# Fused attention and gated convolution on one core: first batch loaded in six-token rows, 120-query tiles, 48-row last tiles, and another written-out order

## The chip, the cores and the metric

The kernel runs on one core of a Trainium2 chip. The metric is device time in microseconds (us), lower is better. Three timed runs of the kernel before gave 172.52, 176.39 and 176.44, median 176.39. One further execution was profiled.

A core has TensorE (PE; its weight loads stand in the profile as PEld), VectorE (DVE), ScalarE (ACT), GpSimd (POOL), which here mostly issues DMAs that convert fp32 to f16 on the way, and SyncE (SP), which only issues DMAs. Each works through its own list in order; semaphores join them.

## The reference

```python
def _attn_ref(q, k, v, n_global, n_local):          # 4 x 8 heads x 768 x 64; 8 global keys, window 96
    scores = scale * np.matmul(q, k.transpose(0, 1, 3, 2))
    rel = pos[:, None] - pos[None, :]
    is_global = pos[None, :] < int(n_global)
    is_local = (rel >= 0) & (rel < int(n_local))
    dist = np.where(is_global & ~is_local, float(n_local), np.abs(rel).astype(np.float32))
    scores = np.where(is_global | is_local, scores - slopes[:, None, None] * dist, -1e9)
    a = np.exp(scores - np.max(scores, axis=-1, keepdims=True))
    return np.matmul(a / (np.sum(a, axis=-1, keepdims=True) + 1e-09), v)

def _moe_ref(x, w_proj, filter_fft, w_out):         # x: 4 x 768 x 512, the heads side by side
    x1, x2, x3 = np.split(x @ w_proj, 3, axis=-1)
    X2 = np.fft.rfft(x2, n=S, axis=1)
    Hf = np.fft.rfft(filter_fft, n=S, axis=0)[None]
    return (x1 * np.fft.irfft(X2 * Hf, n=S, axis=1) * x3) @ w_out
```

Attention keeps a key if it is among the first 8 or at most 95 positions back, with a slope per head times the distance. Its output is projected to x1, x2 and x3; x2 is convolved along the sequence with a filter, multiplied by the other two, and projected again.

## The kernel before

**Tiles of attention.** Keys are cut into seven tiles (`K0`). A tile has 128 partitions: the 8 global keys and 120 keys of its own (`KL`). Tile 6 begins at token 648, so that it is full; only its last 48 keys are new. Scores are computed transposed, keys on partitions and queries along the row. Key tile m meets the queries from 120m on, 216 of them (`EW`: 168 and 48 for the last two). `QT` holds the queries of a batch as one row of 768 per head pair, `KT` the keys by tile and head pair. `scores` (L671) makes two matmuls per tile and head pair, one per head, each on 64 rows of the array (L693). The tiles come in three groups c (`GRP`: tiles 0-1, 2-3, 4-6), so a batch has 12 score operations (4 head pairs by 3 groups), each followed by one exponential on ACT over 864 elements (L707). `values` (L727) multiplies by V with a column of ones, DVE takes reciprocals and scales (`xn`, L766), `transpose_x` (L776) turns the result into `xT`.

**The bias.** In batch 0 it is added by matmuls ahead of the scores (L684): `slope` (diagonals with the heads' slopes) times `near` (distances, spread from `dg`, which POOL makes with iota and affine_select in `distances`, L475). In batches 1 to 3 DVE multiplies the exponentials by `mask` (L724), eight tables of 648 that ACT makes once (L543).

**How q and k come in.** For batch 0, SP loads q as fp32, six tiles of 128 queries into `ot`; PE transposes them as fp32 (`turned32`, L633). POOL loads k and V by `load_run`, one DMA per tile of 960 pieces of 256 bytes (120 keys by 8 heads). For batches 1 and 2, POOL loads q, k and V (`load_rows`, `load_q`, L322), and PE transposes tiles one or two at a time (`turned`, L645). For batch 3 (`CROSS`), SP transposes from buffer to buffer by DMA: three for k, by group, and six for q (`crossed`, L620). All batches share `qn`, `kn`, `QT` and `KT`, so a load waits until the batch before has been transposed.

**The convolution.** `gate` (L846) makes x1 and x3 (two times four matmuls of 384 columns, L856), an eviction of each on ACT or DVE, and their product on DVE. `butterfly` (L794) combines thirds of `xT`; projections (L925), forward transforms (L613), products on DVE, inverse transforms (L950, L953) and the output projection (L977) follow. `ot` is the eviction of the output and SP stores it (L985), one DMA of 128 x 512 fp32 per tile.

**Setup.** DVE builds `rows` (integers 0 to 127 and multiples) by doubling; PE makes angles from them and ACT sines (`tables`). Slopes are 16 ACT operations on 64 x 64 diagonals (L528). DVE fills ones and zeros.

**The order.** `ORDER` is a list written out by hand. Each word is the number of an operation in the order in which `graph` makes them, the engine that runs it (P, A, V, G for POOL, S for SP) and the PSUM banks that it takes; `i13b1` are 13 filler matmuls on `idle` into bank 1. Eight banks exist; an operation that takes a bank waits for all that read the bank's last contents. Each engine works through its own words in this order.

Of the kernel before, what the change touches and what calls it, by code (L numbers as in the profile page):

```python
# [39 lines left out]
0V 42V 3V 7V 27S 59S 28S 60S 61S 26S 69S 4G 54A 48A 45A 56A 50A 5V 1V 6V 29G 30G 66G 33G 65G 77G i6b1 17P0 18A  # L40
58A 47A 46A 43A 19V 11V 12P1 13A 49A 44A 57A 2A 14V 8V 15V 16A 55A 53A 20V 34V 39A 21A 51A 52A 22A 36A 37A 10V
40V 35G 70G 71G 72G 32G 68G 67G 73G i15b3 120P2 121V 9V 41V 93P3 94A 97P1 98V 82V 38V 258G 31G 74G 75G 267G
266G 226P0 95P4 96A 99A 230A 100P5 i1b6 122P2 123A 87A i1b1 126P3 127V 231V 269G i2b1 124P4 125V 101V 62V 64V
229V 268G 257G 255G 256G 259G 79G 76G 78G 80G 81G 262G i2b1 128P67 129A 134P23 135A 91P1 92V 24V 63V 132P45
133A 130P67 131A 102P23 103A 168P1 169V 227V 106P45 107A 170P6 171V 232V 166P7 167A 172P1 173V 228V 25V 261S
260S 263S 264S 275G 274G 273G 272G 265G 104P23 105A 108P45 109A 176P67 177A 178P01 179A 86A 136P23 137V 138V
141P45 142V 143V 174P67 175A 83A 115P23 116V 117V 110P01 111V 112V 180P45 181A 139P6 140A 89A 88A 144P7 145V
182P23 183V 184V 118P0 119A 85A 113P1 114V 187P45 188V 189V 383P7 185P6 186A 84A 384A 385P2 386V 213V 152P3
190P4 191V 212V 219V 215V 220V 357P6 147P2 149A 358A 154A 355P5 356V 198P4 200A 90A 359P2 360V 222V 214V 488G
271G 270G 496G 487G 489S 484G 495G 485G 193P7 195A 162P3 164A 396P01 397A 398V 216V 221V 364P45 361P67 362A  # L50
365A 208P2 210A 151P3 153V 366V 223V 23V 224V 225V 217V 146P0 148A 161P1 163A 165V 150V 218V 157P4 159A 370P67
393P23 394A 395V 367P01 368A 371A 192P5 194V 369V 372V 196V 156P4 158A 160V 155V 363V 233V 234V 235V 236V 237V
238V 239V 297P2 295P3 296A 387P01 388A 298A 390P67 280P4 281A 293P3 294A 391A 207P0 299P1 308P2 309A 300A
306P3 307A 301P5 203P4 205A 302A 284P2 285A 431P1 429P3 430A 432A 202P4 204V 209V 433P5 434A 490S 504G 486G
277G 503G 501G 276G 278G 506G 502G 494G 498G 378P67 379V 380V 392V 389V 252P23 253A 254A 240P4 241V 244P1 245A
246P5 247A 248P67 250A 249A 242P0 243A 373P23 374V 375V 206V 211V 719G 282P1 435P45 436A 283A 399P67 400V 401V
251V 441P23 442A 197P0 199A 404P45 405V 310V 406V 722G 491G 493S 720S 492S 381P1 382V 376P6 377A 288P7 289A
402P2 403V 443V 286P0 287A 583P3 407P4 408A 585P5 586V 437V 290V 584V 291V 303V 438P67 439A 440V 304V 292V
444P01 587P2 588A 445A 446V 311V 715G 717S 716G 409P4 419P5 410P6 412A 421A 420P7 595P23 596A 422A 598P01 599A
425P6 424P5 426A 427A 411A 447P23 448V 305V 449V 611P7 612A 723G 497G 279G 452P01 453V 454V 728G 505G 714G  # L60
500G 659P6 660A 324P5 314P4 315A 320P7 321V 428V 600V 312P2 316P3 317A 325A 313A 450P6 661P4 662A 318P0 455P3
456V 423V 201V 451V 478V 477V 413V 597V 479V 326P5 327A 319A 322P7 415P1 417A 323A 589P23 592P45 593A 811S
414P6 416A 468P0 470A 590A 458P1 460A 613P7 614V 418V 480V 328V 329V 481V 482V 594V 330V 483V 331V 591V 332V
457P6 459A 657P0 658A 729G 507G 734G 713G 712G 499G 730G 726G 727G 725G 732G 731G 724G 735G 733G 473P2 475A
618P45 619A 620V 333V 335V 621P67 615P01 616A 622A 463P3 472P2 474A 462P4 464A 465A 512P5 513A 521P6 522A
669P01 670A 624P23 625A 626V 525P7 526A 523P6 524A 672P45 663P01 664A 508P2 509A 673A 601P67 602V 334V 603V
623V 336V 665V 617V 671V 510P3 511A 467P0 536P1 537A 666P45 667A 668V 838S 718S 814S 813S 812S 837S 882S 721S
839S 883S 340P2 341A 469A 514P1 516P3 517A 515A 632P67 604P2 534P0 535A 538V 633V 674V 527P4 528A 605A 343P3
344A 606P01 607V 634V 608V 518V 352P5 353A 354S 529P4 530A 675P23 676V 519V 471V 635P5 636A 677A 627P67 609P4
610V 680P01 681V 628V 629V 532V 682V 531V 539V 520V 533V 346P5 337P4 338A 347A 339S 345S 342S 348S 349P6 630P7  # L70
631A 821P23 824P01 825A 350A 822A 351S 678P4 679V 826V 683P5 638P7 640A 684A 705V 653P0 548P6 546P1 547A 549A
550P2 544P3 554P7 555A 551A 545A 552P4 553V 706V 708V 707V 466V 461V 709V 476V 542P1 543A 655A 686P5 688A
691P4 693A 643P2 645A 540P3 541A 556V 843P67 840P01 841A 849P45 850A 647P2 649V 637P3 639A 844A 652P0 654V
823V 557V 558V 710V 559V 842V 560V 641V 711V 701P1 703A 893P45 846P23 847A 894A 815P67 736P0 737A 816A 817V
648P1 650A 749P2 890P45 891A 750A 696P3 698A 762P0 763A 832P67 833V 563V 651V 834V 561V 848V 892V 564V 753P1
754A 642P4 644A 751P5 752A 887P23 888A 884P01 818P67 819A 820V 845V 851V 895V 656V 740P4 741A 764P5 738P2 739A
885A 765A 766V 695P3 697A 700P4 742P2 743A 827P67 828V 829V 889V 886V 562V 757P0 758A 580P5 581A 702A 744P1
685P0 687A 755P5 756A 830P4 831A 745A 857P23 858V 859A 896P67 897V 898V 901P45 902V 903A 746V 747V 760V 689V
568P0 565P1 852P67 853V 854V 759V 748V 767V 571P2 572A 577P3 578A 860P4 690P5 861V 761V 835P2 836A 566A 855P3
856A 904P6 905A 899P7 900V 927V 926V 646V 929V 928V 930V 931V 704V 932V 574P2 575A 576S 567S 573S 582S 768P1  # L80
782P4 770P6 771A 569A 570S 579S 774P3 780P2 778P7 779A 783A 769A 868P6 776P0 777A 775A 772P7 773A 781A 784V
785V 786V 699V 787V 788V 791V 862P4 950P1 951A 933P7 934A 692A 694V 789V 792V 937P0 948P1 949A 938A 946P5
935P7 936A 947A 954P1 955A 867P0 952P3 959P5 961P7 962A 869A 953A 960A 872P1 874V 957V 956V 958V 963V 964V
941P2 942A 864A 870A 917P7 939P0 940A 943V 944V 945V 802P1 803A 805P5 878P6 863P4 865A 877P0 980P1 981V 866V
790V 971P4 972A 919A 879A 880A 808P3 984P4 978P2 982P7 983A 979A 967P1 968V 985V 986V 965P0 966A 969P6 970A
973V 881V 974V 975V 987V 976V 988V 977V 1004V 989V 799P7 793P4 794A 800A 801S 795S 804S 873P6 875A 809A 876V
871V 916P2 918A 796P1 797A 991V 990V 992V 993V 994V 920V 1006V 798S 810S 921P4 912P0 914A 911P3 913A 806A 923A
807S 922P2 906P1 908A 924A 925V 915V 907P3 909A 910V 1007V 1005V 1001P0 1002A 1003S 995P1 996A 997S 998P2 999A
1000S 1008P0 1009V 1010S 1014P1 1015V 1016S 1011P3 1012A 1013S
# [108 lines left out]
class Fused:  # L198
# [11 lines left out]
    CROSS = (3,)  # L210
    LATER = ()
# [8 lines left out]
    def __init__(self, ctx, tc, q, k, v, n_global, n_local, w_proj, filt, w_out, out):  # L220
# [10 lines left out]
        self.K0 = [KL * t for t in range(6)] + [S - KL]  # L231
# [6 lines left out]
    def buffers(self):  # L238
# [5 lines left out]
        self.qn = t("qn", [P, 6, H, D])  # L244
        self.kn = t("kn", [P, 7, H, D])
        self.vn = [t(f"vn{i}", [P, 7, H, self.VD]) for i in range(2)]
        self.QT = t("QT", [P, 4, S])
# [4 lines left out]
        self.xn = [t(f"xn{i}", [P, 2, 7, 2, D]) for i in range(2)]  # L252
# [12 lines left out]
        self.h1 = t("h1", [P, 6, DM])  # L265
        self.h2 = t("h2", [P, 6, DM])
# [24 lines left out]
        self.wide_dg = self.mix.bitcast(BF16).rearrange("p a b c -> p (a b c)")[:, 0:648]  # L291
        self.cst = t("cst", [1, 4])
        self.one = t("one", [1, P])
# [31 lines left out]
    def load_rows(self, what, dst, src, b, t):  # L325

        lo, hi = self.K0[t], self.K0[t] + KL
        self.load("G", dst[P - (hi - lo):P, t, :, 0:self.D],
                  src[b, :, lo:hi, :].rearrange("h p d -> p h d"), [what + (t,)], (8 * (hi - lo), 256),
                  f"load{what}{t}")  # L330

    def load_run(self, what, dst, src, t, n):

        rows = src[0, :, self.K0[t]:self.K0[t] + KL * n, :].rearrange("h (t p) d -> p t h d", t=n)
        self.load("G", dst[NG:P, t:t + n, :, 0:self.D], rows, [what + (i,) for i in range(t, t + n)],
                  (8 * KL * n, 256), f"load{what}{t}")

    def load_q(self, b, t):
        src = self.q[b, :, P * t:P * t + P, :].rearrange("h p d -> p h d")
        if b == 0:  # L340
            st = self.ot[t].rearrange("p (h d) -> p h d", h=self.H)
            self.load("S", st, src, [("ot", t)], (1024, 256), f"q{t}")
            if self.Q32:
                return
            self.g.op("AV", {"A": act(512), "V": 0.7}, lambda e: self.copy(
# [26 lines left out]
    def setup(self):  # L372
# [6 lines left out]
        def rows(_):  # L379
            row = self.row  # L380
            v.memset(row[:, 4, 0:1], 0.0)
            for n in (1, 2, 4, 8, 16, 32, 64):
                v.tensor_scalar(row[:, 4, n:2 * n], row[:, 4, 0:n], float(n), None, op0=Alu.add)
# [857 lines left out]
```

## Time and profile before

| | |
|---|---|
| timed runs | 172.52, 176.39, 176.44 us (median 176.39) |
| the profiled execution | 173.44 us, span 171.7 us |
| busy: PE, DVE, ACT, POOL | 162.3, 156.7, 151.1, 77.4 us |
| granted TensorE clock, mean | 0.998 |
| first exponential of batch 0 | starts at 17.50 us |
| first gate matmul | starts at 31.2 us |
| last load issued by POOL | ends at 91.6 us |
| last eviction of the output | 167.88 to 168.48 us |

The span runs from the first to the last instruction of the program; the time has a little around it. Times in lines are microseconds from the start of the span. A group's line ends with its count, the busy time in us, the mean of one in ns, and the engine's idle time ahead of them with what ended it. An engine's instructions overlap, so their durations add up to more than the time that they cost; the distance from one start to the next is the cost in a full engine. Lines such as L322 (loads), L306 (copies), L310 and L312 (products with a constant) are helpers' and stand for many places.

### The profile page before, as it was taken

The page shows a single profiled execution, that of the slowest core. Times are in us where ns is not written, and L with a number is a line of the kernel's source. Part 1 is how long each engine was busy: PE and PEld are TensorE (multiplying, and loading weights), DVE is VectorE, ACT ScalarE, POOL GpSimd, SP SyncE. Part 2 cuts the span into 40 slices and gives each one's busy share as a digit, 9 for nine tenths or more (in the row PEclk, how much of TensorE's full clock was granted, in tenths as well). Part 3 has the DMA queues.
Part 4 walks back from the last instruction along what each step waited for, and adds up shares of the span by engine and source line. Part 5 has one row for each costly group of instructions (what it writes and reads, how often), then busy time and mean ns, then how long its engine had stood idle before and what let it go on. Part 6 is the DMA issues. An engine that isn't in the chain of part 4 may idle for free.

```text
span 171.7 us, 4390 instructions
## 1 busy us (share of the span) xinstructions
PE 162.3 (95%) x1675; PEld 102.2 (60%) x1675; DVE 156.7 (91%) x355; ACT 151.1 (88%) x309; POOL 77.4 (45%) x95
## 2 busy tenths in 40 slices
PE   6888899999999979999999999999999999999990
PEld 1365689865464757965455767654576745575540
DVE  7997989989999899999999998999989999999960
ACT  5799999999899979999999999999998986866841
POOL 8999999962499994948993000000000000000000
PEclk9999999999999999999999999999999999999999
DMA  6999999999999999999999996500000360000854
GB/s 127 181 207 151 144 154 146 169 203 187 148 151 142 144 144 135 87 140 137 156 151 134 153 188 199 230 4 0 0 4 0 117 256 0 0 0 28 308 217 186
DMA packets 98077, 22.44 MB, mean 131 GB/s; under 512 B 90808, under 2 KB 94984, under 8 KB 98056
## 3 DMA queue, kind: packets, MB, share of 16 engines
q0 software_dynamic: 80912, 12.14, 100.3%
q1 hardware_dynamic: 17144, 10.02, 22.2%
q8 instruction: 13, 0.21, 0.5%
q14 instruction: 8, 0.07, 0.1%
HBM read 25.84 MB, written 6.29 MB: 187 GB/s over the span
## 4 chain that ended last, share of the span: by engine, by line
PE 72%; DMA 6%; POOL 6%; DVE 6%; ACT 6%; issue 2%; ACTq 0%; DVEq 0%
PE bank L856 23%; PE bank L925 9%; PE bank L977 9%; PE bank L950 5%; PE bank L693 5%; PE bank L613 5%; PE bank L652 4%; DMA QT<-qn 3%; PE bank L787 3%; PE bank L742 3%; DMA qn<-in_q_dram 3%; POOL kn L322 3%; PE bank L747 3%; POOL vn L322 2%; PE bank L684 2%
## 5 line engine op out<-in xcount | busy, mean ns | idle before, releaser
L856 PE MATMUL bank<-xT,w 128*128 128x384 f16 x256 | 47.4, 326 | 0.0
L707 ACT ACTIVATE E<-bank 128x864 f16<-128x864 f32 x48 | 41.4, 917 | 0.7 <-ACT h L310 0.3
L856 PEld LDWEIGHTS <-w 128*128 128x128 f16 x256 | 23.8, 98 | 16.3 <-issue 1.1
L322 POOL DMA_DIRECT2D vn<-in_v_dram x28 | 25.7, 923 | 4.4 <-DMA g<-in_moe_filter_fft_dram 3.9
L322 POOL DMA_DIRECT2D kn<-in_k_dram x28 | 25.9, 934 | 2.7 <-PE bank L856 2.2
L977 PE MATMUL bank<-wo,y 128*128 128x512 f16 x96 | 22.8, 379 | 0.0
L724 DVE TENSOR_TENSOR E<-E,mask 128x864 f16<-128x864 f16 x36 | 20.8, 603 | 0.8 <-ACT E L707 0.8
L322 POOL DMA_DIRECT2D qn<-in_q_dram x18 | 16.3, 917 | 6.1 <-PE bank L652 5.6
L310 ACT ACTIVATE ot<-bank 128x512 f32<-128x512 f32 x22 | 13.3, 618 | 4.6 <-PE bank L977 4.0
L866 ACT CAST g<-bank 128x384 f16<-128x384 f32 x32 | 15.9, 536 | 1.1 <-PE bank L856 0.9
L310 ACT ACTIVATE ab<-bank 128x512 f16<-128x512 f32 x24 | 14.2, 619 | 2.6 <-PE bank L925 2.5
L766 DVE TENSOR_TENSOR xn<-bank,rc 128x512 f16<-128x512 f32 (+1 forms) x21 | 16.0, 764 | 0.5
L742 PE MATMUL bank<-vn,E 128*128 128x65 f16 x224 | 15.3, 193 | 0.0
L742 PEld LDWEIGHTS <-E 128*128 128x128 f16 x224 | 14.0, 97 | 1.9
L747 PE MATMUL bank<-vn,E 128*128 128x65 f16 x192 | 15.1, 193 | 0.0
L977 PEld LDWEIGHTS <-y 128*128 128x128 f16 x96 | 8.9, 98 | 9.3 <-DVE y L1056 0.2
L693 PE MATMUL bank<-QT,KT 64*128 64x216 f16 (+2 forms) x224 | 13.9, 241 | 0.3 <-DMA QT<-qn 0.3
L306 ACT CAST X<-bank 128x512 f16<-128x512 f32 x24 | 13.6, 610 | 0.6 <-PE bank L613 0.5
L310 ACT ACTIVATE x<-bank 128x384 f16<-128x384 f32 x25 | 12.5, 526 | 1.3 <-DVE g L868 1.0
L747 PEld LDWEIGHTS <-E 128*128 128x128 f16 x192 | 13.2, 97 | 0.5
L306 ACT CAST eo<-bank 128x384 f16<-128x384 f32 x27 | 11.5, 508 | 1.4 <-PE bank L953 1.4
L693 PEld LDWEIGHTS <-KT 64*128 64x128 f16 x224 | 8.5, 94 | 6.3 <-issue 4.4
(142 smaller groups left out, 354.8 us busy)
## 6 DMA issues: line engine op xcount, KB each, us to landing
out_dram<-ot SPq DMA_DIRECT2D x24, 256.0 KB
kn<-in_k_dram POOLq DMA_DIRECT2D x28, 120.0 KB, 5.4
vn<-in_v_dram POOLq DMA_DIRECT2D x28, 120.0 KB, 5.2
qn<-in_q_dram POOLq DMA_DIRECT2D x18, 128.0 KB, 5.3
ot<-in_q_dram SPq DMA_DIRECT2D x6, 256.0 KB
w<-in_moe_w_proj_dram POOLq DMA_DIRECT2D x4, 256.0 KB, 6.7
g<-in_moe_filter_fft_dram POOLq DMA_DIRECT2D x1, 768.0 KB, 14.1
w<-in_moe_w_proj_dram POOLq DMA_DIRECT2D x1, 512.0 KB, 9.4
```

The source lines that it names most:

```text
L306: {"A": nc.scalar.copy, "V": nc.vector.tensor_copy, "G": nc.gpsimd.tensor_copy}[e](out, in_)
L310: self.nc.scalar.mul(out, in_, c)
L322: return self.g.op(eng, 0.57 + 0.00035 * nbytes[0] if eng == "G" else 0.5, lambda _: e.dma_start(dst, src), w=w, r=r, nbytes=nbytes, name= ...
L693: nc.tensor.matmul(bs[hh].f32()[:, off:off + w], self.KT[hs, m, hp], self.QT[hs, hp, KL * m:KL * m + w], start=(off == 0 and not near), st ...
L707: g.op("A", act(864), lambda _: nc.scalar.activation(eo, bs[0].two()[:, :, 0:432].rearrange("p h (m w) -> p h m w", m=2), Act.Exp, scale=s ...
L724: g.op("V", dve(864, 2), lambda _: nc.vector.tensor_mul(eo, eo, mk), r=[("mask", 2 * hp), ("mask", 2 * hp + 1)], w=[("E", hp, gi)], name=" ...
L742: nc.tensor.matmul(o[:, n, hh], ef[:, at:at + P], vt[:, t, 2 * hp + hh, 0:D + 1], start=first, stop=(t == 0), skip_group_check=True)
L747: nc.tensor.matmul(o[:, n, hh], ef[:, at:at + P], vt[:, t - 1, 2 * hp + hh, 0:D + 1], start=False, stop=True, skip_group_check=True)
L766: nc.vector.tensor_mul(to, o[:, :, :, 0:D], rc.to_broadcast([P, 2, 2 * nt, D]))
L856: nc.tensor.matmul(bk.f32()[:, 0:h], self.w[:, c, o + P * j:o + P * j + P], self.xT[:, c, h * s:h * s + h], start=(c == 0), stop=(c == 3))
L866: g.op("A", act(h), lambda _: nc.scalar.copy(x3, pts[1].f32()[:, 0:h]), use=[pts[1]], w=[ko], name="x3")
L977: nc.tensor.matmul(bk.f32(), y[:, c, P * t:P * t + P], self.wo[:, c, :], start=(c == 0), stop=(c == 3))
```

## The change

- **Batch 0's q and k by head pair.** `six` takes the place of `turned32` and of `turned` for batch 0. One DMA on POOL (`load_six`) brings both heads of a pair with six consecutive tokens in a partition: 256 pieces of 1536 bytes. There are eight such loads, four for q and four for k. PE makes 12 transposes of 64 columns each, into the two halves of a bank's partitions, and an eviction writes them back in token order, six elements apart, into seven tiles; a second small one writes the last 48. The global keys are copied per head pair (`kg`). SP no longer loads q.
- **120-query tiles.** `QT` becomes seven tiles like `KT`, and q is loaded by 120 rows (`load_q`). A score matmul over 216 queries becomes one over 120 and one over 96 of the next tile. Batches 1 and 2 transpose seven q tiles.
- **48-row last tiles.** Key and value tile 6 begins at token 720 and has 48 rows, at the bottom of the partitions (`R0`). The rows between are set to zero once (`blank`, `ones`).
- **Batch 3's crossing** is two DMA transposes for k (tiles 0-1, 2-6) and two for q (tiles 0-2, 3-6).
- **Slopes** in 8 pieces of 128 rows, on ACT or DVE, from a matrix `two` with 1 in one half of the partitions and 0.5 in the other.
- **The last output tile** is projected, evicted and stored in two halves of 256 columns (`HALVES`).
- **Smaller setup:** `rows` by outer sums; the ones beside V only where they are read; no zeros under the global keys; tables `h1`, `h2` lose unused slots. `XX` is empty, so `crossed_x` isn't run.
- **The order** is another list, 999 operations instead of 1017.

```diff
@@ ORDER (all new; its beginning)
+0V 24V 1V 2A 3V 10V 39V 7V 53S 54A 27G 26G 49G 50G 28G 4G 40V 29G 52G 30G 51G i13b1 12P0 13A 14V 17P1 18A 41A
...
@@ class Fused
-        self.K0 = [KL * t for t in range(6)] + [S - KL]
+        self.K0 = [KL * t for t in range(6)] + [S - 48]
+        self.R0 = [NG] * 6 + [P - 48]
...
-        self.QT = t("QT", [P, 4, S])
+        self.QT = t("QT", [P, 7, 4, P])
...
@@ loads
+    def load_six(self, what, dst, src, i):
+        self.load("G", dst[:, i], src[0, 2 * i:2 * i + 2].rearrange("h (p r) d -> p h r d", r=6),
+                  [(what + "six", i)], (256, 1536), f"six{what}{i}")
...
@@ rows
-            for n in (1, 2, 4, 8, 16, 32, 64):
-                v.tensor_scalar(row[:, 4, n:2 * n], row[:, 4, 0:n], float(n), None, op0=Alu.add)
-            for j in range(4):
-                v.tensor_scalar(row[:, j], row[:, 4], 6.0, float(j), op0=Alu.mult, op1=Alu.add)
+            outer(y.rearrange("p (a b) -> p a b", a=4), x, x, 4)
+            outer(row[:, 4].rearrange("p (a b) -> p a b", a=8), y[:, 0:8], y, 16)
+            v.scalar_tensor_tensor(row[:, 0:4], row[:, 4:5].to_broadcast([1, 4, P]), 6.0,
+                                   x[:, :, None].to_broadcast([1, 4, P]), op0=Alu.mult, op1=Alu.add)
...
@@ distances
+        for hp in range(4):
+            for k in range(2):
+                g.op("AV", {"A": 0.17, "V": 0.16}, lambda e, hp=hp, k=k: self.times(
+                    e, self.slope[:, hp, k, 64 * k:64 * k + 64], two, self.slopes[2 * hp] / self.scale),
...
@@ batch 0's transposes
+        def turn(_):
+            for r in range(6):
+                for hh in range(2):
+                    nc.tensor.transpose(b.f16()[64 * hh:64 * hh + 64, P * r:P * r + P], buf[:, r, hh], self.ident)
...
+        def move(e):
+            self.copy(e, dst[:, 0:6, i, lo:lo + KL].rearrange("p m (c r) -> p r m c", r=6),
+                      view(0, 120).rearrange("p r (m c) -> p r m c", m=6))
+            self.copy(e, dst[:, 6, i, end[0]:end[1]].rearrange("p (c r) -> p r c", r=6), view(120, P))
...
@@ scores
+                for x in range(1 + (w > KL)):
+                    n = w - KL if x else min(w, KL)
+                    for hh in range(2):
+                        hs = slice(64 * hh, 64 * hh + 64)
+                        nc.tensor.matmul(bs[hh].f32()[:, off + KL * x:off + KL * x + n], self.KT[hs, m, hp],
+                                         self.QT[hs, m + x, hp, 0:n], start=(off == 0 and x == 0 and not near),
+                                         stop=True, skip_group_check=True)
...
@@ conv, the output
+            for lo, hi in ((0, 256), (256, 512)) if last and t == 5 and self.HALVES else ((0, 512),):
```

## The prediction

> **What bounds the kernel now.** I read the page's busy shares, then the table by stage, the chain that ended last, and the timelines of ScalarE (ACT), GpSimd's queue (POOL) and SyncE's queue (SP).
>
> ```profile
> PE 162.3 (95%) x1675; PEld 102.2 (60%) x1675; DVE 156.7 (91%) x355; ACT 151.1 (88%) x309; POOL 77.4 (45%) x95
> ```
>
> Three engines are nearly full, so the stage decides which of them counts. In the table by stage the columns are the stretch, its length, then busy time and instructions of PE, PEld, DVE, ACT, POOL, the clock and the DMA figures:
>
> ```profile
> 10.00:15.00 5.00, 3.54 (x37) 2.48 (x35) 3.82 (x14) 4.92 (x15) 4.93 (x8) 1.00 1.71 178
> 15.00:20.00 5.00, 4.53 (x65) 3.01 (x64) 4.55 (x8) 4.97 (x8) 5.00 (x7) 1.00 2.29 146
> ...
> 110.00:120.00 10.00, 10.00 (x90) 5.16 (x88) 9.85 (x21) 9.67 (x17) 0.00 (x0) 1.00 0.01 2
> ```
>
> Up to about 30 us ACT has no idle time and PE has (27 of its matmuls there are fillers on `idle`); later PE has none. The chain (start, length, what) says the same of the end:
>
> ```profile
> 31.21 0.65 PE bank L856 x4
> ...
> 162.62 5.19 PE bank L977 x24
> 167.88 0.60 ACT ot L310
> ```
>
> A busy share overstates PE, whose matmuls overlap, so I price PE's work by distances between starts in the chain: 384 columns 0.163 us, 512 columns 0.216, a 128-column transpose 0.0555, 65 columns 0.030, an fp32 transpose 0.109, one head pair's scores 0.56 with the bias matmuls and 0.185 without, four inverse matmuls 0.33. Over the program's counts that is 256 x 0.163 + (96 + 96 + 48 + 4) x 0.216 + 244 x 0.0555 + 416 x 0.030 + 24 x 0.109 + 12 x 0.56 + 36 x 0.185 + 32 x 0.33 and 1.1 of small ones: **148.3 us**. Added in the order of the list, 17.4 us stand ahead of the first gate matmul, which starts at 31.2, and 130.9 behind it. PE ends at 167.8, so of those 136.6 us only 5.7 are stalls. The kernel is thus an ACT-bound start, a PE-bound stretch of 136.6 us, and a tail of 3.9. Gains come from reaching PE's stretch earlier, from its 5.7 us of stalls, or from the tail.
>
> **The start.** ACT's timeline:
>
> ```profile
> 3.05 1.20 ACT L310 ACTIVATE eo<-ident 64x64 bf16<-64x64 f16 x5
> ...
> 13.32 1.05 ACT L306 CAST QT<-bank 128x512 f16<-128x512 f32 x2
> ...
> 15.56 1.28 ACT L543 ACT_TABLE_LOAD   x1
> ...
> 17.50 4.78 ACT L707 ACTIVATE E<-bank 128x864 f16<-128x864 f32 x6
> ```
>
> The first exponential starts at 17.5. Ahead of it go 16 slope pieces, three `near` spreads, four q evictions and tables. By starts, a slope piece costs 0.25, a spread (216 + 264 elements) 0.66, a 512-element eviction 0.48, an exponential 0.77, a mask 0.645.
>
> After: ACT's list up to the first exponential holds the first V rows 0.48, two `y` 0.76, two sines 0.76, five slope pieces 1.0 (128 rows each, bounded by the 64-row piece at 0.25 above and its fastest, 0.145, below; I take 0.2), one spread 0.66, five six-row evictions, one inverse table 0.28, one copy of global keys 0.11 to 0.29 (I take 0.11) and the exponential's table 1.28. A **six-row eviction** (720 + 48 elements, written six elements apart) is in no row. The 480-element copy at 0.45 and the 1024-element one at 0.90 on ACT give 0.66 + 0.10 = 0.76; if strided writes doubled it, 1.5. I take 0.76, as nothing in ACT's rows depends on layout: 3.8 for five. On DVE (three of them) the rows bound it by 0.59 (480 f16 elements in 0.325) and 1.02 (512 fp32 ones in 0.68); I take 1.0.
>
> [...]
>
> Without the first V rows, which fall into the idle time before, ACT's list is 0.76 + 0.76 + 1.0 + 0.66 + 3.8 + 0.28 + 0.11 + 1.28 = 8.7 us. It can start when `rows` and the angle matmuls are done, at 5.24 now. `rows` shrinks from 3.1 us (1.73 to 4.9) to between 1.6 and 2.3 (nine small operations instead of 16, at the rows' 0.06 to 0.6), but a 0.85 us memset goes ahead: about 4.9. That gives 13.6. DVE bounds it too: `dg` comes later on POOL (behind seven loads and the identity; six-row loads at 0.63 each, on the line through 0.73 for 512 descriptors and 0.90 for 960: 0.7 + 4.4 + 0.6 = 5.7, plus the 4.0 that `dg` took, 9.7), then DVE needs `dg2V`, two spreads, two far rows, about 4.2: 14.0. I take the first exponential at **14.5**, three us sooner.
>
> Twelve exponentials then need 9.3 us: 23.8. But PE's list has the first values after the eighth scores, and values need V's tile 0:
>
> ```profile
> 18.02 2.69 POOL L322 DMA_DIRECT2D vn<-in_v_dram  x3
> ```
>
> V's tile 0 is issued first in this row, and the first values that read it run at 25.9. After, it is the 17th entry of POOL's list: 9.7, one six-row load, two rows of 0.9, two weights of 0.73, `far` 0.6, two V tiles: 15 to 16.1. At the median landing of 5.2 it is there at 20 to 21, when eight exponentials have run (14.5 + 6.2 = 20.7). I allow 1 us of wait: exponentials end at 25. One mask, one paired q eviction (0.9) and six masks follow: 25 + 7 x 0.645 + 0.9 = 30.4. Only then comes the first gate eviction, now at
>
> ```profile
> 33.38 0.61 ACT L866 CAST g<-bank 128x384 f16<-128x384 f32 x1
> ```
>
> PE's list up to the first matmul that needs a bank freed by that eviction (x1 of gate 2) holds 19.5 us, of which 9.6 lie before the first values at 20.7; the other 9.9 fit into 20.7 to 30.6. So at about 30.4 PE has the rest left.
>
> **PE's work.** Removed: 24 fp32 transposes (2.6) and 28 k transposes (1.6). Added: 96 transposes of 64 rows. The only pairs of 64-column outputs in the trace (L460) start together, the next pair 0.08 later, so 48 pairs cost 3.8 (2.7 at the plain rate, 5.3 if none go together). A seventh q tile in batches 1 and 2: 8 x 0.0555 = 0.44. Together 148.4, of which 128.9 remain at 30.4: PE ends at 30.4 + 128.9 = 159.3 plus stalls, against 31.2 + 130.9 = 162.1 plus stalls. **-2.8 us.**
>
> Scores split 216 columns into 120 and 96, 96 pairs more. Pairs of 216, 168 and 48 columns start 92, 72 and 24 ns apart, a straight line with 2 to 4 ns at zero: +0.2, or +2.3 if each extra pair costs what the smallest one does. I take **+0.2**.
>
> **Stalls.** Of the 5.7, one is named: a transpose of x waits 1.0 us for DVE's `xn` near 60. By the lists, ACT loses about 0.9 us of work over the program and DVE 1.6 (shorter memsets and `rows`, fewer key evictions, against spreads and strided evictions). Loads shrink: the first batch's k goes from 6720 packets to 1024, and each last tile from 960 to 384. I take **-0.5**, between -3 (half of them gone) and +4 (another order meets other waits).
>
> **Tail.** The last eviction now takes 0.60 us after its matmuls; of 256 columns, 0.38: -0.2. The second store of the tile is issued behind the first on SP, which costs nothing while the first half's runs ahead by its 0.43 us; without that cover it adds one issue, about 0.7. I take **-0.3**, with 0.1 for the shorter transfer.
>
> Sum: -2.8 + 0.2 - 0.5 - 0.3 = **-3.4 us**. The profiled execution took 173.44 (span 171.7), which gives 170.0. The three timed runs reach from 172.52 to 176.44 with the median 176.39; by ratio the same sum gives 172.9 there. I predict **172.0**, between the two.
>
> **Rivals.**
> (1) The start gains nothing: V's tile 0, now behind a burst of 3.1 MB and the weights, lands only at 24. ACT then starves after eight exponentials, the last four end at 28, the masks at 33.4. The 2.8 are gone: 172.8 by the profiled execution, **174.8** with the same two us on top as in the forecast. For it: POOL issues without a pause in this stage. Against: 5696 fewer packets ahead.
> (2) The strided evictions cost double: 3.8 us on ACT before the first exponential. 173.8 by the profiled execution, **175.8**. Against: ACT's rows price only elements.
> (3) **Slower:** batch 3's crossings. SP and POOL now:
>
> ```profile
> 89.71 1.85 POOL L322 DMA_DIRECT2D vn<-in_v_dram  x2
> ...
> 90.94 5.27 SPq L629 DMA_TRANSPOSE QT<-qn  x3
> 96.39 4.07 SPq L626 DMA_TRANSPOSE KT<-kn  x2
> ```
>
> Nine transposes take 15.2 us for 13 tiles, and scores of group 1 need few. After, they need q tiles 3 to 6 and k tiles 2 to 6 in two pieces, each waiting for its last load, the k piece queued behind the q piece. With POOL ending near 89 the last k lands at 95; nine tiles at 1.17 make 105.5, about when PE gets there (30.4 + 71.6 of work + 3 of stalls = 105). If POOL ends at 91.6 as now and a tile costs 1.76 (three in 5.27), it is 97 + 15.8 = 113: 8 us of wait, 178 by the profiled execution, **180**. It decides from about 3.4 us of wait on.
>
> **Chances.** Forecast 0.60, rival 1 0.18, rival 2 0.07, rival 3 0.15. A measurement tells about 2% from no change, that is 172.9 and 179.9. Of the forecast's own spread (168 to 174.5) four fifths lie below 172.9: 0.48, with 0.02 from rivals 1 and 2 faster 0.50; slower 0.13, as rival 3 mostly ends over the line; same 0.37. The range takes in the stalls' lower end (170.0 - 3 = 167) and rivals 1 and 2 with room: 166.5 to 177.5, leaving out rival 3 and little else.
>
> **What would show it.** First exponential near 14.5 and the last of batch 0 near 25; first gate eviction near 30; six-row evictions 0.76 apart on ACT; scores' pairs 52 and 42 ns apart; PE without waits on QT or KT near 100 to 106; last matmul near 164.5. I am wrong if ACT waits long between exponentials of batch 0, or if the stalls behind 30 us exceed 8 us.

## The result and the profile after

The changed kernel takes **181.81 us** (median of 4 runs, 181.69 to 182.22). The kernel before, over four runs, takes 174.45 (172.39 to 176.44). Two of these four, at 176.4, fell into a slower state, and the ratio is taken against the other two, at 172.39 and 172.52. The ratio is **1.055, interval 1.052 to 1.058**: slower, where 172.0 and a gain were forecast, and outside the range. The profiled execution took 182.22 with a span of 180.4; before it was 173.44 and 171.7, so 8.8 us have to be found.

The page after, with the busy share of PE and the granted clock in forty slices of 4.5 us:

```profile
PE 164.0 (91%) x1910; PEld 106.2 (59%) x1910; DVE 157.0 (87%) x362; ACT 156.8 (87%) x299; POOL 75.2 (42%) x99
PEclk9995586999999999999999999999999999999999
```

PE has 1.7 us more busy time than before, ACT 5.7, DVE 0.3. The clock, full throughout before, falls to 0.5 to 0.8 in the four slices from 13.5 to 31.6 us. The table by stage (stretch, length, busy time and instructions of PE, PEld, DVE, ACT, POOL, then clock and DMA) puts the trouble in the start:

```profile
10.00:15.00 5.00, 1.06 (x17) 0.71 (x12) 2.93 (x16) 5.00 (x6) 4.93 (x8) 0.77 1.32 151
15.00:20.00 5.00, 2.49 (x32) 1.71 (x33) 2.97 (x3) 5.00 (x9) 1.38 (x2) 0.50 1.67 139
...
110.00:120.00 10.00, 10.00 (x110) 6.62 (x108) 9.82 (x18) 9.67 (x20) 0.00 (x0) 1.00 0.38 143
```

ACT is busy all the time in the first two rows, as before, but with 6 and 9 instructions in place of 15 and 8, and PE beside it does 1.06 and 2.49 us instead of 3.54 and 4.53. In the stretch from 110 us PE is full, as before. What ACT does in those ten us is in its timeline (start, length, instruction, count, idle time ahead and what ended it):

```profile
7.06 0.87 ACT L420 ACTIVATE y<-bank 128x512 f32<-128x512 f32 x2 [4.05 <-PE bank L451]
...
9.65 2.71 ACT L315 COPY KT<-bank 128x720 f16<-128x720 f16 x2
...
12.47 2.70 ACT L315 COPY QT<-bank 128x720 f16<-128x720 f16 x2
...
15.60 2.71 ACT L315 COPY QT<-bank 128x720 f16<-128x720 f16 x2
...
18.15 2.79 ACT L315 COPY KT<-bank 128x720 f16<-128x720 f16 x2
...
21.39 2.71 ACT L315 COPY KT<-bank 128x720 f16<-128x720 f16 x2
24.12 1.28 ACT L728 ACT_TABLE_LOAD   x1
25.41 4.20 ACT L728 ACTIVATE E<-bank 128x864 f16<-128x864 f32 x5
```

Each pair is one six-row eviction, a copy of 720 elements and a small one of 48. The 720 alone take 2.54 to 2.63 us on ACT and 2.54 to 2.57 on DVE; the forecast had 0.76 for both copies together. The first exponential starts at 25.41 (17.50 before). The chain that ended last (start, length, what) shows the same copies:

```profile
1.19 5.30 PE bank L311 x13
...
12.57 2.61 ACT QT L315 x2
...
21.88 2.75 DVE KT L315 x3
25.41 0.90 ACT E L728
```

Its first piece is 13 fillers on `idle`, 0.41 us each; ACT's wait of 4.05 us for the angles ends right behind them. The line that the forecast put at 30.4 us, the first gate eviction (33.38 before), is now

```profile
42.14 0.84 ACT L904 CAST g<-bank 128x384 f16<-128x384 f32 x2
```

From there on the two kernels take the same time. This eviction comes 8.76 us later than before; from it to the start of the last matmul it is 133.8 us (134.0 before), and from that matmul to the end of the span 4.5 (4.3 before). **8.76 - 0.21 + 0.22 = 8.77, the whole difference.** The slow third rival, batch 3's crossings, isn't in it: POOL's last load of V starts at 94.66, the four transposes by DMA run from 86.19 to 106.7 on SP (the last three are shown), and no wait of PE on `QT` or `KT` out of a transpose appears among the waits of the trace.

```profile
90.49 11.81 SPq L639 DMA_TRANSPOSE QT<-qn  x2
102.52 4.15 SPq L631 DMA_TRANSPOSE KT<-kn  x1
```

### The profile page after: what moved, and what is told of

Its sections match the earlier page's. It is cut to its first block, busy times and chain, and to the rows that moved or that the text cites. A ratio compares the mean times of both kernels' runs of the same rounds, so it can differ in the third digit from the quotient of the medians.

```text
span 180.4 us, 4839 instructions
## 1 busy us (share of the span) xinstructions
PE 164.0 (91%) x1910; PEld 106.2 (59%) x1910; DVE 157.0 (87%) x362; ACT 156.8 (87%) x299; POOL 75.2 (42%) x99
## 4 chain that ended last, share of the span: by engine, by line
PE 84%; ACT 8%; DVE 3%; issue 2%; DMA 1%
PE bank L894 24%; PE bank L966 12%; PE bank L1021 10%; PE bank L715 6%; PE bank L617 6%; PE bank L991 5%; PE bank L765 4%; PE bank L679 4%; PE bank L817 4%; PE bank L770 3%; PE bank L704 3%; PE bank L311 3%; ACT QT L315 3%; ACT KT L315 2%; DVE KT L315 2%
## 5 line engine op out<-in xcount | busy, mean ns | idle before, releaser
L894 PE MATMUL bank<-xT,w 128*128 128x384 f16 x256 | 48.5, 326 | 0.0
L331 POOL DMA_DIRECT2D kn<-in_k_dram x25 | 21.5, 865 | 18.2 <-PE bank L679 12.2
L331 POOL DMA_DIRECT2D vn<-in_v_dram x28 | 24.7, 894 | 0.5 <-PE bank L715 0.3
L1021 PE MATMUL bank<-wo,y 128*128 128x512 f16 (+1 forms) x100 | 23.2, 371 | 0.0
L331 POOL DMA_DIRECT2D qn<-in_q_dram x25 | 21.5, 865 | 1.0 <-DMA w<-in_moe_w_proj_dram 0.4
L319 ACT ACTIVATE x<-bank 128x384 f16<-128x384 f32 x30 | 15.1, 521 | 3.9 <-PE bank L894 2.8
L715 PEld LDWEIGHTS <-KT 64*128 64x128 f16 x416 | 12.0, 98 | 6.5 <-issue 4.7
L715 PE MATMUL bank<-QT,KT 64*128 64x120 f16 (+2 forms) x416 | 15.4, 211 | 0.0
L319 ACT ACTIVATE ot<-bank 128x512 f32<-128x512 f32 (+1 forms) x22 | 12.6, 598 | 3.2 <-PE bank L1021 2.7
L1021 PEld LDWEIGHTS <-y 128*128 128x128 f16 x100 | 9.4, 98 | 8.6
```

The costliest lines, as they stand in the source:

```text
L319: self.nc.scalar.mul(out, in_, c)
L331: return self.g.op(eng, 0.57 + 0.00035 * nbytes[0] if eng == "G" else 0.5, lambda _: e.dma_start(dst, src), w=w, r=r, nbytes=nbytes, name= ...
L715: nc.tensor.matmul(bs[hh].f32()[:, off + KL * x:off + KL * x + n], self.KT[hs, m, hp], self.QT[hs, m + x, hp, 0:n], start=(off == 0 and x ...
L894: nc.tensor.matmul(bk.f32()[:, 0:h], self.w[:, c, o + P * j:o + P * j + P], self.xT[:, c, h * s:h * s + h], start=(c == 0), stop=(c == 3))
L1021: nc.tensor.matmul(bk.f32()[:, 0:hi - lo], y[:, c, P * t:P * t + P], self.wo[:, c, lo:hi], start=(c == 0), stop=(c == 3))
```

## The experiments

Three things could have made the start late: the order in which the evictions write, the slow clock beside them, and the fillers. All kernels below are the changed kernel with the edit shown; lines behind L660 can be up to three further on.

**The eviction read the other way round.** The same elements go to the same places, but the copy runs through them in the order of the target: writes are consecutive, reads from PSUM 128 elements apart. The small copy of 48 is turned round in the same way.

```diff
-            self.copy(e, dst[:, 0:6, i, lo:lo + KL].rearrange("p m (c r) -> p r m c", r=6),
-                      view(0, 120).rearrange("p r (m c) -> p r m c", m=6))
+            self.copy(e, dst[:, 0:6, i, lo:lo + KL].rearrange("p m (c r) -> p m c r", r=6),
+                      view(0, 120).rearrange("p r (m c) -> p m c r", m=6))
...
```

> The eight six-row evictions walk the same elements in another order: token by token, so that the writes are consecutive and the reads from PSUM are 128 elements apart. Theory: the cost of 2.55 us for 720 elements comes from writing 2-byte elements 12 bytes apart; the copy falls to 0.7 to 1.0, five of them on ACT give back 8 us, the first exponential moves from 25.4 to 16 to 17.5 and the time from 181.8 to about 173.5. Rival A: the cost comes from the four-level pattern or from f16 in PSUM; the copy stays at 2.5 and the time at 181.8. Rival B: the time is lost to TensorE's granted clock of 0.5 to 0.8 between 10 and 30 us; the copies get short, but the time stays above 178.

172.14 us (171.41 to 173.16), ratio to the kernel before 0.997, interval 0.994 to 1.000. ACT's timeline of this kernel, the lines that answer to those above:

```profile
10.02 0.84 ACT L315 COPY KT<-bank 128x720 f16<-128x720 f16 x2
...
11.07 0.86 ACT L315 COPY QT<-bank 128x720 f16<-128x720 f16 x2
...
16.96 9.50 ACT L729 ACTIVATE E<-bank 128x864 f16<-128x864 f32 x12
```

A pair takes 0.84 instead of 2.71 us, the 720 elements 0.74 to 0.78 on ACT and 0.89 to 1.04 on DVE: the sizes that the forecast had taken. The first exponential comes 8.45 us sooner and the profiled execution is 9.06 us shorter. By starts, the five pairs on ACT cost 0.73 to 0.89 each and 3.8 in all, the forecast's own figure; in the changed kernel they cost 12.1. The order in which these copies write accounts for the whole loss. Reading 128 elements apart costs ACT nothing (0.74 to 0.78 us here, 0.76 for a copy consecutive on both sides, below), and the clock is 9 again in all slices but one, though nothing was done about it.

**One eviction twice.** If ACT and DVE set the start, a repeated copy must arrive at the end in full. For two head pairs the copy of q is made a second time, into the same place.

```diff
+            if i < 2 and what == "q":
+                self.copy(e, dst[:, 0:6, i, lo:lo + KL].rearrange("p m (c r) -> p r m c", r=6),
+                          view(0, 120).rearrange("p r (m c) -> p r m c", m=6))
```

> Two of the eight evictions of 720 elements are made twice, q of head pair 0 on ACT and q of head pair 1 on DVE; the result is the same. Theory: each stands on the way to the first exponential and everything behind it is shifted: first exponential 2.4 us later, near 27.8, time 2.4 us up, near 184.2. Rival: the start has slack behind the evictions (loads of V, masks, TensorE's clock), and the time rises by less than 1 us.

184.13 us, one execution, against 181.81. ACT's part of it moved the first exponential by 2.47 us to 27.88, the first gate matmul from 39.80 to 41.59 and the last matmul by 1.8. The row with three copies in place of two:

```profile
12.49 5.14 ACT L315 COPY QT<-bank 128x720 f16<-128x720 f16 x3
```

ACT's list has no slack ahead of the exponentials. Of the 2.5 us added there 1.8 reach the end of PE and 1.9 the span. The missing 0.7 need not be slack: the changed kernel's own trace has a pause of PE among the first values that this one lacks,

```profile
35.62 0.19 PE L770 MATMUL bank<-vn,E 128*128 128x65 f16 x1 [1.05 <-issue]
```

and the profile names no cause for it ("issue").

**Does the clock cost?** PE's idle time is filled with 27 more matmuls, put where it waits for the evictions.

```diff
-91P1 92A 207P2 208A 93A 84P3 85V 209V 210V 86P0
+91P1 92A i8b6 207P2 208A i8b6 93A 84P3 85V 209V 210V i8b6 86P0
...
-99P45 100A 96P1
+99P45 100A i3b6 96P1
```

> The changed kernel as it is (strided evictions, 13 fillers), with 27 more filler matmuls in the waits of TensorE between 12 and 25 us, so that its granted clock stays up. Theory: ACT and DVE set the pace there, and the clock of 0.5 to 0.8 is a consequence of TensorE's waits and costs under 0.7 us: time within 0.7 of 181.8. Rival: the low clock is a cause of its own and takes 1.5 us or more of the 8.8: time at or below 180.3.

181.60 us (180.86 to 181.96), ratio 1.049 with 1.045 to 1.053. The table by stage has the clock at 1.00 up to 20 us, where it was 0.77 and 0.50, and 0.96 in the next five, where it was 0.70. But over 25 to 30 us, where exponentials of batch 0 run, it is 0.50, lower than the changed kernel's 0.66:

```profile
15.00:20.00 5.00, 3.65 (x35) 1.78 (x34) 2.63 (x2) 5.00 (x6) 2.35 (x4) 1.00 1.69 131
...
25.00:30.00 5.00, 4.54 (x60) 3.77 (x61) 4.12 (x7) 4.54 (x6) 5.00 (x6) 0.50 1.60 134
```

The first exponential comes 0.9 us sooner, the first gate matmul only 0.1 (39.68): ACT's waits for scores between these exponentials grow from 0.2 to 1.0 us. The fillers have moved the slow stretch, not removed it, so this run does not tell what the changed kernel takes at full clock. The next one comes closer.

**Fewer fillers.** Six instead of 13 ahead of the angles.

```diff
-0V 24V 1V 2A 3V 10V 39V 7V 53S 54A 27G 26G 49G 50G 28G 4G 40V 29G 52G 30G 51G i13b1 12P0
+0V 24V 1V 2A 3V 10V 39V 7V 53S 54A 27G 26G 49G 50G 28G 4G 40V 29G 52G 30G 51G i6b1 12P0
```

> The 13 filler matmuls ahead of the angle matmuls become 6, as before the change. Theory: fillers take 0.43 us each there, so 13 of them end at 6.5 and hold the angles back, and ACT's first table work with them (7.1 instead of 5.2); with 6 the angles run at 4, ACT starts its list 2 to 3 us earlier, and as ACT then has no gap up to the first exponential the time falls by about 2, to 180. Rival: the list waits for another thing at the same moment (loads, identity, slopes); the time falls by less than 0.5.

180.01 us (179.77 to 180.52), ratio 1.040, interval 1.033 to 1.047. In PE's timeline the fillers end, and the first matmul of the angles starts, 2.6 us sooner:

```profile
1.19 2.74 PE L311 MATMUL bank<-idle 128*128 128x512 f16 x6 [1.19 <-DVE idle L375]
3.87 0.60 PE L444 MATMUL bank<-eo 1*128 1x512 f16 x1
```

ACT's first `y` starts at 4.93 instead of 7.06, the very 4.9 that the forecast had. Of these 2.1 us the first exponential gets 1.4 (24.02), the first gate matmul 2.1 (37.67); the pause of 1.05 us among the first values isn't in this trace either, so the last 0.7 need not be the fillers'.

This kernel also bounds what the clock costs. Its evictions are as slow as in the changed kernel (pairs of 2.71 to 2.79 us on ACT), and over 15 to 20 us PE is as idle beside them (2.45 us busy, 2.49 there), yet its clock is 1.00 in every stage of the start, where it was 0.50:

```profile
15.00:20.00 5.00, 2.45 (x33) 1.76 (x34) 2.46 (x3) 5.00 (x8) 2.54 (x4) 1.00 1.74 139
```

With fewer fillers and a full clock together the time is still 4% above the kernel before. One of its four executions had a mean clock of 0.941 and took 180.52 us, the others 0.990 to 0.998 and 179.77 to 180.02. By these executions a slow clock costs under 0.8 us, of a loss of 8.8. What sets it isn't shown: in this stage PE was as idle with it as without it.

**Both edits.**

> Both mends together: row-wise evictions and 6 fillers ahead of the angles. Theory: the two parts stand one behind the other on ACT's list, so their gains add: first exponential near 15 (17.0 with the evictions alone), time near 170.4, 1.2 to 1.5% under the kernel before. Rival: with short evictions DVE's chain of identity, distances and spreads ends last, and 6 fillers give less than 0.5 us more: 171.8.

**171.45 us (170.77 to 171.67), ratio 0.990, interval 0.987 to 0.994**: about one per cent faster than the kernel before, the fastest of this study by its median. The first exponential is at 15.19. But 1.8 us gained there against the row-wise kernel have become 0.5 at the first gate matmul (29.24 against 29.78). ACT's timeline says where:

```profile
15.19 6.37 ACT L729 ACTIVATE E<-bank 128x864 f16<-128x864 f32 x8
22.83 3.39 ACT L729 ACTIVATE E<-bank 128x864 f16<-128x864 f32 x4 [1.26 <-PE bank L716]
```

Behind eight exponentials ACT waits 1.26 us for scores, which stand behind the first values in PE's list; these start at 21.6, V's first tiles being issued at 13.58 to 15.4 us. This is the place of the first rival.

**The last tile whole**, on top of both edits.

```diff
-    HALVES = True
+    HALVES = False
...
-987P7 988A 989S 993P6 994A 995S 996P5 997A 998S
+987P7 988A 989S 993P6 994A 995S
```

> As the last one, with the last output tile projected, evicted and stored whole. From the profiles the tail from the last start of a matmul to the end of the span was 4.3 before, 4.5 to 4.7 with halves. Theory: the first half's store is issued only 0.6 us after its eviction has ended, behind the second eviction, and the second store 0.44 later, so the halves lose: whole is faster by 0.2 to 0.6 us. Rival (the forecast): halves gain 0.3, whole is slower by 0.3.

171.57 us (171.26 to 172.24), ratio 0.992, interval 0.989 to 0.996. That is the time with halves. From the last matmul's start to the end of the span it is 4.58 us whole and 4.45 in halves: the forecast's 0.3 for this part is not there to be seen.

**The first values' loads ahead.** In the whole-tile kernel, V's first two loads are issued ahead of the gate's weights, and in this first try also ahead of the two selections on POOL that make the far rows (32G).

```diff
-239G 66G 32G 38V 83V 64G 79P3 80A 45A 33A 35V 236G 58G 57G 89P0
+239G 58G 57G 32G 66G 38V 83V 64G 79P3 80A 45A 33A 35V 236G 89P0
```

> Row-wise writes, six fillers and whole last tile, as in the run before it; the two loads of the first values are issued ahead of one load of gate weights, the last two loads of gate weights ahead of them and one load of queries no longer (13.58 and 14.48 us become about 10.6 and 11.5). Theory: when the evictions were mended and the fillers cut, the first exponential came 1.8 us earlier but the time fell only 0.7 us, because the first values land at 20.5 to 21.5 us and ACT waits 1.3 us after its eighth exponential for scores that stand behind them. Then ACT's wait goes, the twelfth exponential starts at 24.0 to 24.4 us (25.36 before), the first gate matmul comes 0.7 to 1.3 us earlier (29.27 before) and the ratio to the kernel before is 0.984 to 0.990 (0.992 before). Rival: behind the values stand the masks and the weights of the gate; then the twelfth exponential comes earlier, but the first gate matmul stays within 0.3 us of 29.3 and the ratio at 0.992.

172.84 us (171.60 to 174.64), ratio 0.997, interval 0.993 to 1.001: nothing gained, and neither case was right. The far rows came 1.05 us later, DVE waited for them, and so ACT waited 1.67 us after its first exponential:

```profile
17.74 0.89 ACT L729 ACTIVATE E<-bank 128x864 f16<-128x864 f32 x1 [1.67 <-PE bank L716]
```

The wait had been moved from the ninth exponential to the second. With the far rows ahead again:

```diff
-239G 66G 32G 38V 83V 64G 79P3 80A 45A 33A 35V 236G 58G 57G 89P0
+239G 32G 58G 57G 66G 38V 83V 64G 79P3 80A 45A 33A 35V 236G 89P0
```

> As the kernel with the first values ahead of one load of gate weights, but with the two selections that fill the far rows (0.62 us of POOL) put back ahead of these values: in that kernel they had come 1.05 us later, at 12.37, and ACT waited 1.67 us for its second exponential. POOL is to run: one load of queries and keys, the far rows at about 10.6, the first two values at 11.2 and 12.1 (13.58 and 14.48 in the whole-tile kernel), then both loads of gate weights. Theory: the second exponential follows the first at once (16.1 us), the values land by about 19, the wait of 1.3 us after the eighth goes, the twelfth exponential starts at 24.0 to 24.6 (25.36 in the whole-tile kernel), the first gate matmul at 28.0 to 28.7, and the ratio to the kernel before is 0.982 to 0.990. Rival: the masks, the values' own reading order or the gate weights hold the first gate matmul at 29 or later, whenever the values land; the ratio is 0.990 to 0.996.

171.80 us (171.22 to 173.87), ratio 0.994, interval 0.989 to 0.999. ACT now runs its twelve exponentials without a wait, and the twelfth starts at 24.05 instead of 25.36:

```profile
15.57 9.51 ACT L729 ACTIVATE E<-bank 128x864 f16<-128x864 f32 x12
```

The theory's first half holds, its second doesn't: the first gate matmul comes at 28.96, only 0.3 us sooner, and the ratio can't be told from that of the whole-tile kernel. PE's timeline names the next in the row, the loads of V behind the first two:

```profile
24.73 0.20 PE L766 MATMUL bank<-vn,E 128*128 128x65 f16 x1 [1.05 <-DMA vn<-in_v_dram]
```

The chain that ended last runs through this landing (6.63 us from the end of the issue). So rival 1 had its mechanism right, though not its size: in this stage the loads of V arrive just in time, one after the other (1.26 us of wait behind the first two in the kernel with both edits, 1.05 us for a later one here). That they alone hold the gain at about a us is likely but not shown, as no run issues the later ones sooner.

**What the eviction's price depends on.** Behind all other work the row-wise kernel makes extra copies of 720 f16 elements, on DVE and then on ACT; their results are read by nobody, so only single durations count. The first kernel varies the step of the writes, then the source and the type.

```diff
+            for r in (2, 3, 6, 12):
+                self.copy(e, to[:, 0:720].rearrange("p (c r) -> p r c", r=r),
+                          ps[:, 0:720].rearrange("p (r c) -> p r c", r=r))
+            self.copy(e, to[:, 0:720], ps[:, 0:720])
+            self.copy(e, to[:, 0:720].rearrange("p (c r) -> p c r", r=6), ps[:, 0:720].rearrange("p (r c) -> p c r", r=6))
+            self.copy(e, to[:, 0:720].rearrange("p (c r) -> p r c", r=6), sb[:, 0:720].rearrange("p (r c) -> p r c", r=6))
...
```

> The rowwise kernel with 20 extra copies behind the last output, ten forms on DVE and ten on ACT, each of 720 elements (360 where the source is fp32): f16 out of PSUM into f16 2, 3, 6 and 12 elements apart, consecutive, consecutive writes with reads 120 elements apart, the step of 6 out of SBUF, the step of 6 into fp32, fp32 into fp32, and SBUF to SBUF with strided reads. Only durations of the copies are read; they go to a buffer that nothing reads. Theory of the writes: all forms with steps of 2 and more into f16 cost about 2.5 on both engines, the same with an SBUF source, and consecutive writes 0.5 to 1.0 whatever the reads. Rival: the reads decide, or only the step of 6 or 12 is slow, or only one engine.

The timeline behind the kernel's own work; in this order writes of step 2, step 6, consecutive, consecutive with reads 120 apart, step 6 out of SBUF, and step 6 on ACT:

```profile
165.77 0.95 DVE L315 COPY E<-bank 128x720 f16<-128x720 f16 x1 [3.30 <-PE bank L1159]
...
168.14 2.54 DVE L315 COPY E<-bank 128x720 f16<-128x720 f16 x1
...
174.07 0.53 DVE L315 COPY E<-bank 128x720 f16<-128x720 f16 x1
174.63 0.91 DVE L315 COPY E<-bank 128x720 f16<-128x720 f16 x1
175.57 1.36 DVE L315 COPY E<-X 128x720 f16<-128x720 f16 x1
...
182.16 2.54 ACT L315 COPY E<-bank 128x720 f16<-128x720 f16 x1
```

The price grows with the step, against the theory's one price for all: 0.95, 1.35, 2.54 and 3.31 us for steps of 2, 3, 6 and 12, equal on both engines to a few ns. Consecutive writes take 0.53 on DVE and 0.76 on ACT. Into fp32, step 6 costs 1.53 and 1.62. "Whatever the reads" holds for PSUM alone: out of SBUF, consecutive writes with reads 120 apart take 0.79 on DVE but 1.51 on ACT. The second kernel asks for what the price is paid, with steps of 4, 8 and 24, and with runs of consecutive elements.

```diff
+            for r in (4, 8, 24):
+                self.copy(e, to[:, 0:720].rearrange("p (c r) -> p r c", r=r),
+                          ps[:, 0:720].rearrange("p (r c) -> p r c", r=r))
+            for t in (2, 4, 8):
+                self.copy(e, to[:, 0:720].rearrange("p (c r t) -> p r c t", r=6, t=t),
+                          ps[:, 0:720].rearrange("p (r c t) -> p r c t", r=6, t=t))
```

> Row-wise writes; after all work twelve extra copies of 720 elements of 2 bytes each, on DVE and ACT in turn, from consecutive elements in PSUM into SBUF, whose results nobody reads: steps of 4, 8 and 24 elements, and runs of 2, 4 and 8 consecutive elements with the next run 12, 24 and 48 elements on. The four steps measured before (2, 3, 6, 12: 0.95, 1.35, 2.54, 3.31 us) fit one price for each stretch of 16 bytes that a write enters: 180, 270, 540 and 720 of them, 4.6 to 5.3 ns each. Theory (a price for each 16 bytes entered): step 4 takes 1.7 to 1.8 us, steps 8 and 24 3.3 us both, runs of two 1.7 to 1.8 us (360 entered), runs of four 0.85 to 0.95 us, runs of eight 0.76 us on ACT and 0.5 to 0.6 us on DVE. Rival (a price for a 4-byte word that is half written): runs of two write whole words, and take 0.8 us or less; step 24 takes what step 12 takes.

Step 4, step 8, and runs of two with the next run 12 elements on:

```profile
167.40 1.75 DVE L315 COPY E<-bank 128x720 f16<-128x720 f16 x1 [3.29 <-PE bank L1158]
169.18 3.33 DVE L315 COPY E<-bank 128x720 f16<-128x720 f16 x1
...
176.02 0.79 DVE L315 COPY E<-bank 128x720 f16<-128x720 f16 x1
```

For single elements the theory holds: 1.75, 3.33 and 3.44 us for steps 4, 8 and 24. All seven steps fit 4.6 to 5.3 ns for each 16 bytes that a write enters (180, 270, 360, 540, then 720 of them). For runs of elements it fails, and the rival's price is met: runs of two, each a whole 4-byte word, take 0.79 on both engines where 1.7 was expected, and runs of four 0.53 on DVE, like consecutive ones. So in these copies single 2-byte elements pay (0.95 to 3.44 us, against 0.53 on DVE and 0.76 on ACT for consecutive ones), and runs of two and more, which write whole words, much less (0.53 to 0.79). That is a fit to these copies; what happens inside the memory isn't shown, and why DVE out of SBUF pays 1.36 instead of 2.54 stays open.

## Why the prediction was wrong

**The step that failed is the price of a six-row eviction.** It was taken at 0.76 us on ACT, "as nothing in ACT's rows depends on layout", with 1.5 as the upper bound, and at 1.0 on DVE, bounded by 0.59 and 1.02. It is 2.55 us for the 720 elements on both. The rows used as bounds were all of copies whose writes I took to be consecutive, and the 1.5 was no row at all but a doubling picked by hand. By starts, as the forecast counts, the five pairs on ACT cost 2.33, 2.32, 2.34, 2.42 and 2.73 us, 12.1 in place of 3.8: 8.3 more. The angles, below, are 2.2. Together 10.5, and the first exponential came 10.9 us after the 14.5 of the forecast.

The copies behind all other work show how far from a doubling it is: on DVE, step 2 takes 1.8 times the consecutive copy (0.95 us against 0.53), step 4 3.3 times (1.75) and step 6 4.8 times (2.54); on ACT, whose consecutive copy takes 0.76, step 4 takes the same 1.75 and step 6 the same 2.54.

**Rival 2** ("the strided evictions cost double") had the right mechanism and place. Its size was short: 3.2 times on ACT, not 2. With 8.3 us in place of its 3.8, its 173.8 by the profiled execution becomes 178.3, and the 2.2 of the angles bring 180.5, where 182.22 was measured. It stood at 0.07, and the chance of a slower kernel rested mostly on rival 3.

**The start of the angles.** "About 4.9" came from `rows` alone. The 13 fillers that stand ahead of the angles in PE's list were not priced: 13 x 0.41 = 5.3 us from 1.19 on, so 7.06. With six of them it is 4.93.

**The last exponential of batch 0** ("25", with 1 us allowed for V): in the kernel with both edits it ends at 26.2, having waited 1.26 us; with V's first loads ahead it ends at 25.1. The forecast's first exponential (14.5) is 15.19 there. Rival 1, at 3 us of wait, was too large; the wait itself was real, but in the changed kernel the slow evictions gave V time to land.

**PE's stretch.** From the first gate eviction to the last matmul the forecast has 128.9 + 0.2 + 5.2 = 134.3 us. It is 133.8 after and 133.9 with both edits, 134.0 before. Work and stalls together were sized within half a us; the step "-0.5" of stalls can't be told from nothing. But the 5.7 us called stalls were mostly not waits: behind the first gate eviction the traces have 1.5 us in which PE is idle before and none after; the rest is work priced too low, or pauses too short for the profile to show. (The products as printed add up to 148.1, not 148.3; it makes no difference to the -2.8.)

**Split scores** (+0.2): eight pairs of 120 and 96 columns and what follows take 487 ns where four pairs of 216 took 476. That is 2.8 ns for each of 96 added pairs, 0.27 us in all.

**Tail** (-0.3): 0.2 longer after. The halves show no gain.

**Rival 3**, the crossings: no wait. In the kernel with both edits, too, where they run from 75.7 to 97.9 us, PE never waits for them.

The sum of -3.4 thus rested on a gate eviction at 30.4 instead of 33.38. In the kernel with both edits it is at 31.59 and the profiled span 1.8 us shorter than before; with V's loads ahead it is at 31.30 and the span 2.2 us shorter. The plan was worth about half of the forecast or less (by the timed ratios 1.7 and 1.0 us of 3.4), once its evictions wrote in order and six fillers stood where it had thirteen.

## What to carry to other kernels

Read an access pattern for the order of its writes: out of PSUM into SBUF, single 2-byte elements cost 4.6 to 5.3 ns for each 16 bytes entered in these copies of 128 x 720, on ACT and DVE alike, while the same permutation out of PSUM with consecutive writes and scattered reads is free on ACT (0.76 us per 720 either way) and costs 0.91 instead of 0.53 us per 720 on DVE. Where no row shows an operation's form, a bound taken from another form is no bound; keep the slower side open, and price the fillers in front of a chain like all else. When a stage is mended, look up the next transfer that arrives just in time, and when you move one load forward, check what it is moved past.

## What the runs showed that was not expected

- DVE and ACT take equal times for scattered 2-byte writes out of PSUM (0.954 and 0.955 us at step 2, 2.543 and 2.542 at step 6, 3.311 and 3.311 at step 12), though consecutive ones differ (0.53 and 0.76). One limit outside both engines would look like this, but DVE's 1.36 us out of SBUF, below, doesn't fit it; the cause stays open.
- DVE copying at step 6 out of SBUF takes 1.36 us, out of PSUM 2.54; ACT takes 2.58 out of SBUF.
- PE's granted clock fell to 0.50 over 15 to 20 us in the changed kernel, where PE was busy half of the time (2.49 of 5 us). With six fillers in place of thirteen it stayed at 1.00 there, with PE no busier (2.45). With 27 extra matmuls it was 1.00 there, and 0.50 over 25 to 30 us instead.
- A filler of 512 columns costs 0.43 us from start to start up to 5.9 us in the changed kernel, against 0.216 later, though the clock column of the table reads 1.00 in these first stages too. In the kernel with 27 extra matmuls the step from 0.43 to 0.216 comes at 4.1 us.
